# Threshold attention and a max-out FFN on one core: 29 half tiles are masked by GpSimd, and the written order is made anew

## The chip, the cores and the metric

The kernel runs on one core of one Trainium2 chip. The core has a matrix engine (TensorE, PE in the profile; its weight loads are listed apart as PEld), VectorE (DVE), ScalarE (ACT), GpSimd (POOL) and a queue engine (SyncE, SP) that here issues nearly all DMAs. All engines run their own instruction queue in order and wait for each other through semaphores. The metric is the device time of one execution in microseconds; lower is better.

## The reference, cut to what matters

```python
# q, k, v: (8, 8, 576, 64); x: 4608 tokens x 512; d_ff = 768
scores = q @ k.T / sqrt(64)                     # per batch and head, 576 x 576
thresh = max(scores, axis=-1) - tau             # tau = 0.02
scores = where(scores >= thresh, scores, -1e9)
attn   = exp(scores - max(scores)) / (sum + 1e-9)
attn_out = attn @ v
x = attn_out.transpose(0, 2, 1, 3).reshape(4608, 512)
h = max(x @ w1, x @ w2, x @ w3)
out = h @ w_out
```

Every row of a 576 x 576 score matrix keeps only the entries within tau of its maximum; the others get weight zero.

## The kernel before, in words

**Tiling.** A batch has two quads of four heads; the 16 quads run one after the other. A quad's scores are made in 9 steps of two half tiles each, so there are 288 half tiles of 128 rows x 576 columns, float32, each in one of four PSUM slots of two banks. Each half tile is a letter S in the written order. Quads' q and k are loaded (l), transposed on TensorE (T) and copied out (a on ScalarE, c on VectorE); GpSimd makes a copy of q with the partition halves exchanged (q). A finished quad gives products with v (O, copied out by w and x), and a finished batch goes through the FFN: 18 hidden pieces (six blocks of d_ff by three weights; F starts one, B is its second half) whose running maximum is made by h on ScalarE and v on VectorE, then output pieces (F, B again; copied out by u, stored by o) and the piece of the ninth rows (N, j, i). The last batch is cut in two parts (SPLIT), and its last output is copied by VectorE (f) and stored from ScalarE's queue (d).

**What happens to a half tile.** Letter m, VectorE: one pass from PSUM into a buffer z in SBUF, negated, with the row minimum nm collected, that is minus the row maximum. Then it depends on the digit of the half tile in the table MASKED:

- kind 0: s, VectorE, 128 x 1: threshold th = max - tau. e, ScalarE: Prelu(z + th) with a slope of 2^-100 for what is kept, so that kept entries are tiny and the others are large. n, ScalarE: Exp with scale -2^100, the sum collected.
- kind 1: e, ScalarE: Exp(-z + nm). k, VectorE: one pass that keeps what is at least exp(-tau) and sums it.
- kinds 2 and 3 are 0 and 1 with e reading the scores from PSUM.

When both halves of a step have their sums, r takes the reciprocals (VectorE), p normalizes each half into the bfloat16 tile P (GpSimd, one pass per half), and t transposes P through a DMA into ptq for the products.

**Buffers.** z has nine buffers of its own and, from half tile 72 on, two of eleven are taken from the two weight-staging tiles ("stage" in the profile). P has six. hm, the running maximum of the FFN, has three.

**Order.** ORDER is a text in which each letter issues one step; S, T, O, F and N carry the PSUM slot. Each engine gets its instructions in the order of this text, and `_Ordered` fixes that order. So the text decides what stands ahead of what in each queue. It is written by a planner outside the kernel, which is not shown. Nearly all instructions go through one helper, so the profile puts them on line 93; they are told apart by tile names: sc scores, z and stage the half tiles, P, ptq, tp transposes, qt, kt, qs the operands, o products, xt their copies, ph hidden pieces, hm and hT, po output pieces, ob their copies.

Of the kernel before, what the change touches and what calls it, by code (L numbers as in the profile page):

```python
# [21 lines left out]
FLAT = 2.0 ** -100  # L22

MASKED = """
220202110002002100110000100020020312000112012010100000000010100000001100
001000111010000101100000000000110001100000011110110200100000100010000000
110001101110100100010000001001100100000100101111102300000100100000001000
001000110100100001000000000100100001011110100011011100002100001000001013
"""


# [6 lines left out]
SPLIT = {7: ((0, 1), (2, 3, 4))}
# [3 lines left out]
ytS1erkpT2agmnT3pclesqS2aqetS0meqlrnspmS1eqsT2nmpS3tnrcS0zlemS2eprmS3npmtS0npsgS1sermpS2emyS3eptmT0eplmS1ayl  # L42
meS0kynS2tssT3snkynkercperlT3pmnpmntqremS0lasprgeT3pmeS2psstnplnS0mzecesqrmS3etqkeS2gpnmS1npsmtnS0prmleS3pmS
2npsmnS0yrsmetperS2epmO1eqtnkplemnzswT2teS3rplS1empnmS3tpnssrS1klepS0mapermtS2epmT1S3nmqtnkO2qemncpS3txrskT1
peS2rmeS0ptmegpamS2npS1ertsmpnlkzS2elmS3eS0mpnlO1srkepsmnO2tyeprgwnpmT1xS3cpeS0sszmF2eS1meBqkF0ngqT3shrsmBay
S2tvpnF3rpemS1BpemF0pnsvT2BnyctS1esrlsT2mphS3lezS1maF0myntpT2sS3ngrcqF1eBmpnS2svpBnrmS3peS0tmeyF2zmnF3lBsvep
S0rhkBptesF2mgeS1zvF0nsmBpteBsrgvpnF1kS3phS2semBnqmF0S3evqF2ntrmBpelS1spvBnlmS3qhF0rsmepS1tnBpsmS3ezvS2eS1rm
pF0etsyO3mnlkngpO2eswetkBxrmpT3nF2rvpaS1BnqmS0hspS3meF2prS1smntBzesmF3ezvT0tBeclT1yS2pnvS0apsmtS3eyrmlS1epS2
mepF0mnqsmnS3tkBnkeF1restpkumeS2prtBumlperkpS0ustS2umS3pesmS1eqtT0mO2nlpceqsrmO3ntywelkS0pxlS1meF3prnS2smBye
myF0thpskS1oeBpF2nlvF3nlrmBpeBkpS1hstsvS0eF3lrmpnF2mBepBsveF1nT0vBtarkS3lhqS2smleF0prF1mnBysntBveS2plvnS0pom  # L50
F3nyS1pmeBsysmF0thT2rrlpeS1clF3epsmBnqT2svBaS1evqS2nmF0pS3nmqBtnmT2pS1hrcpS3esmS0petF2melS1rmpBnF3skpetF0sve
BlBmnF2vhtF1esrBkpnS0vtT3npBmS2arvpS0ermO3eqtsmepT1swntpS0cF2epesmtnS3kT1nS0mtBessrkpameS3preS1mS0uqmuS3mpnS
1tsmS2pnoS0rempS3lempO1lnkqlemO2lnymeO0srkpetkeF3swxykxpT2BercnprtS1uyS2upmF0termqS3eBymN2lhsskpelkS0eF3ertm
S1pjBlmeS0plvF2npS1mnyF3tpmnBsopT0nvBaS1kF2ieqrssmS0hlpBmelT1qF3snrvF0epcBlepS2vBnpsmtS1nS3rmphS2mnpF1smeS0B
snmF3tevS2T0mF1atBrsekpBevS0thS2pmF3nymS1qeBrsmnpS0tvF2eplF1rmnpBskeBptF3hsvS0eBrsstpmnS1lvT2qeO0mpnlscnT3wS
1etF2srramS0lnqBmlF3eqvT1nBcpS0thF2pemS1perS3mpBnmS0ptesO1smpnkteF3yvxT0BraktyS2esS1vpeS0mpnS3meqF2mnyrmpnT0
# [12 lines left out]
ynwtprmopS0xmpS2emF3peS1mteBrsmpS0nF2pmhtS1nkBS3evF0nstmN2erkpeF1mBjpsBevS2hskF0eF3rkpteBmF1nBpveBkO2hsrvpeS
0rtwS1pnmF2npmS3eBympF1ntrvS0epBmpS2rF3svtpeS0mnpS1sBmiF2smhF0ntkBBervpS1etF3smpnF2BervpS1hsBpnmF0tevS3F1nmB  # L70
etrBkpO2vhO3nspS1xrwepS0mpF3smS2etF1snmBeBstvnS2S0veS3meF1snkeF2rmpnmpeBnkBerrptukpuO3rN1xpuO0jpuO3wptF1xpF2
hF0tvF1vF3hF0vtF1vF2hF0viF1vF2ohF0voF1vF3hF2vF1vF3hF2vO1vO0wF2xF3F1huF0vF3vF2ohF1vF3vF2hF0vF1vF3hF0vF2vF3hF1
vF2vF0hF1vF2vF0uF1ouN0ofjdi
"""


# [28 lines left out]
def kernel(  # L105
# [273 lines left out]
    def exponents(c, r):  # L379
        z = c["z", r]  # L380
        src, sign = (c[r], -1.0) if direct(c, r) else (z, 1.0)
        if masked(c["g"], c["idx"], r):
            scalar.activation(out=z, in_=src, func=AF.Exp, bias=c["nm", r], scale=-sign)
        else:
            th = c["nm", r] if direct(c, r) else c["th", r]
            scalar.activation(out=z, in_=src, func=AF.Prelu, bias=th, scale=sign, alpha=FLAT)

    def numerators(c, r):
        z, acc = c["z", r], c["sm"][:, r:r + 1]
# [89 lines left out]
    def ffn(b, part):  # L479
# [219 lines left out]
    def flow(what, fn):  # L699
        while True:  # L700
# [7 lines left out]
    line = {k: [] for k in "menkrptahvuxwcqsjf"}  # L708
# [10 lines left out]
    def issue(what, where):  # L719
# [27 lines left out]
        elif what == "m":  # L747
            c, r = line["m"].pop(0)
            maximum(c, r)
            line["e"].append((c, r))  # L750
            if not masked(c["g"], c["idx"], r) and not direct(c, r):
                line["s"].append((c, r))
        elif what == "s":
            threshold(*line["s"].pop(0))
        elif what == "e":
            c, r = line["e"].pop(0)
            exponents(c, r)
            line["k" if masked(c["g"], c["idx"], r) else "n"].append((c, r))
        elif what in "nk":
            c, r = line[what].pop(0)  # L760
            if "sm" not in c:
                c["sm"] = small.tile([128, 2], F32, name="sm")
            else:
                c["summed"] = True
# [65 lines left out]
```

## Time and profile before

| | before |
|---|---|
| time, median of 3 runs | 442.97 us (442.29 to 443.37) |
| the profiled execution: span from first to last instruction | 440.2 us |
| TensorE busy, share of the span | 418.9 us, 95% |
| VectorE | 393.9 us, 89% |
| ScalarE | 403.6 us, 92% |
| GpSimd | 317.0 us, 72% |
| mean granted TensorE clock | 0.988 |

The profile gives the execution's span; what lies around it is not in the profile, and the median of the runs is 2.77 us above the span. "Busy" is time in which an engine executes an instruction; matmuls are pipelined and their ends are modelled. A row of the stretches has an engine's busy time in that stretch and, in brackets, its instructions. A row of the waits names who waited, for whom, the total in us, how often, and the longest. A row of a group of instructions has count, busy time, mean duration in ns, and the idle time before them with what ended it. A row of the timeline has start, length, engine, line, operation, output and inputs, and the count of like instructions merged into it.

### The profile page before, as it was taken

To read this page: it belongs to the slowest core of one execution; us is meant where nothing else is said; L and a number is where in the kernel's file an instruction comes from. 1 tells how busy PE (TensorE), PEld (TensorE's weight loads), DVE (VectorE), ACT (ScalarE), POOL (GpSimd) and SP (SyncE) were. 2 spreads that over 40 slices of the span, in tenths; PEclk is the share of its full clock that TensorE was granted. 3 is DMA by queue.
4 is the path that set the end of the run, shared out by engine and by line. 5 is a ranking of instruction groups with operands and counts; after the bars stand their busy time and mean duration, and the time that the engine had idled before them with its cause. 6 is when DMAs were issued, how large, how long until landed. Compare 5 with 4: busy or idle time off the path is not lost.

```text
span 440.2 us, 14283 instructions
## 1 busy us (share of the span) xinstructions
PE 418.9 (95%) x5188; PEld 313.6 (71%) x5190; DVE 393.9 (89%) x1248; ACT 403.6 (92%) x834; POOL 317.0 (72%) x420
## 2 busy tenths in 40 slices
PE   7696789999999999999999999999999999999996
PEld 6353446787788776787678777887688777786873
DVE  4888899999999999999999999999889999998542
ACT  4999999999999999999999999999999998989521
POOL 1988999998787778867786778886585776554400
PEclk9987999999999999999999999999999999999999
DMA  6999999999999999999999999999698778583812
GB/s 190 276 239 214 270 215 260 263 252 252 220 277 224 237 165 242 291 160 232 189 242 238 202 182 273 192 199 208 135 237 153 147 109 185 102 169 72 192 50 85
DMA packets 213959, 88.50 MB, mean 201 GB/s; under 512 B 189184, under 2 KB 202240, under 8 KB 213888
## 3 DMA queue, kind: packets, MB, share of 16 engines
q1 hardware_dynamic: 213360, 86.96, 95.4%
q8 instruction: 41, 0.67, 0.6%
q10 hardware_dynamic: 528, 0.62, 0.5%
q14 instruction: 30, 0.25, 0.2%
HBM read 35.65 MB, written 9.44 MB: 102 GB/s over the span
## 4 chain that ended last, share of the span: by engine, by line
PE 78%; DVE 5%; POOL 5%; issue 4%; ACT 3%; DMA 2%; SPq 1%; DVEq 0%; POOLq 0%; ACTq 0%
PE ph L93 31%; PE sc L93 26%; PE po L93 10%; PE o L93 8%; POOL P L93 4%; PE tp L93 3%; ACT z L93 3%; DVE z L93 3%; DMA qm<-in_q_dram 2%; SPq L93 1%; DVE kt L93 1%; POOL w L93 1%; DVE stage L93 0%; DVE hm L93 0%; POOL qs L93 0%
## 5 line engine op out<-in xcount | busy, mean ns | idle before, releaser
L93 POOL TENSOR_SCALAR P<-z,rs 128x576 bf16<-128x576 f32 x250 | 202.0, 819 | 59.1 <-DVE rs L93 30.4
L93 DVE TENSOR_SCALAR_CACHE_REDUCE z<-sc 128x576 f32<-128x576 f32 x250 | 183.2, 749 | 12.2 <-PE sc L93 8.1
L93 PE MATMUL sc<-kt,qs 64*128 64x256 f32 (+2 forms) x640 | 179.8, 417 | 5.5 <-DVE z L93 3.9
L93 PE MATMUL sc<-kt,qt 64*128 64x320 f32 (+2 forms) x640 | 180.9, 429 | 3.1 <-DVE z L93 1.2
L93 PE MATMUL ph<-xt,w 64*128 64x288 bf16 (+2 forms) x2160 | 172.0, 283 | 0.2 <-DVE hm L93 0.2
L93 PEld LDWEIGHTS <-w 64*128 64x128 bf16 (+1 forms) x2160 | 128.0, 94 | 31.6 <-issue 4.0
L93 ACT ACTIVATE z<-z,th 128x576 f32<-128x576 f32 x161 | 120.5, 767 | 2.2 <-DVE th L93 1.9
L93 ACT ACTIVATE z<-z 128x576 f32<-128x576 f32 x175 | 117.6, 674 | 0.2
L93 PEld LDWEIGHTS sc<-kt,qs 64*128 64x128 f32 (+1 forms) x640 | 92.4, 179 | 22.5 <-DVE z L93 8.6
L93 PEld LDWEIGHTS sc<-kt,qt 64*128 64x128 f32 (+1 forms) x640 | 92.0, 179 | 14.7 <-DVE z L93 3.5
L93 DVE SCALAR_TENSOR_TENSOR z<-z 128x576 f32<-128x576 f32 x75 | 61.7, 827 | 1.4 <-ACT z L93 1.1
L93 POOL COPY qs<-qt 64x640 f32<-64x640 f32 (+3 forms) x66 | 45.9, 695 | 19.5 <-ACT qt L93 16.1
L93 ACT ACTIVATE z<-z,nm 128x576 f32<-128x576 f32 x72 | 53.9, 767 | 0.0
L93 PE MATMUL po<-wo,hT 64*128 64x512 bf16 (+3 forms) x454 | 53.3, 354 | 0.3
L93 DVE TENSOR_TENSOR hm<-ph,hm 128x576 bf16<-128x576 f32 (+2 forms) x54 | 37.0, 685 | 9.8 <-PE ph L93 9.6
L93 ACT ACTIVATE hm<-ph 128x576 bf16<-128x576 f32 (+2 forms) x54 | 31.9, 590 | 14.3 <-PE ph L93 13.8
L93 PEld LDWEIGHTS <-hT 64*128 64x128 bf16 (+2 forms) x456 | 28.4, 95 | 18.5 <-issue 2.6
L93 DVE TENSOR_TENSOR hT<-ph,hm 128x576 bf16<-128x576 f32 (+2 forms) x54 | 36.9, 683 | 2.8 <-PE ph L93 1.0
L93 PE MATMUL o<-ptq,vb 128*64 128x512 bf16 (+2 forms) x544 | 38.7, 282 | 0.2 <-DVE z L93 0.2
L93 POOL TENSOR_SCALAR P<-stage,rs 128x576 bf16<-128x576 f32 x38 | 29.5, 783 | 11.7 <-DVE rs L93 8.4
L93 ACT ACTIVATION_READ_ACCUMULATOR z<-z 128x1 f32 x175 | 33.6, 192 | 0.0
L93 PEld LDWEIGHTS <-vb 128*64 128x64 bf16 x544 | 22.4, 111 | 14.0 <-issue 5.6
(44 smaller groups left out, 412.2 us busy)
## 6 DMA issues: line engine op xcount, KB each, us to landing
vm<-in_v_dram SPq DMA_DIRECT2D x32, 256.0 KB, 4.6
qm<-in_q_dram SPq DMA_DIRECT2D x15, 512.0 KB, 4.7
km<-in_k_dram SPq DMA_DIRECT2D x15, 512.0 KB, 5.4
out_dram<-ob SPq DMA_DIRECT2D x14, 512.0 KB, 4.5
stage<-in_moe_w_dram SPq DMA_DIRECT2D x9, 512.0 KB, 5.6
ptq<-P SPq DMA_TRANSPOSE x144, 4.5
vr<-in_v_dram SPq DMA_DIRECT2D x16, 128.0 KB, 3.8
stage<-in_moe_w_out_dram SPq DMA_DIRECT2D x3, 512.0 KB, 5.5
```

The lines of the kernel that those rows point to most:

```text
L93: ins = fn(*a, **kw)
```

## The change

29 half tiles get a new kind, 4. For it m and s are as for kind 0. Then GpSimd makes two passes: b computes (z + th) * 2^100 and writes it as 8-bit integers to the upper byte of each element of a bfloat16 tile "far" whose lower bytes are zero, so that an element is either a very large number or minus zero; C adds far to z. G, ScalarE, is then a single Exp(-z + nm) with the sum collected. There is one far tile. The table MASKED and the whole text ORDER are new; they were made by the planner with instruction fetches taken into account and with larger random late landings of DMAs. hm has two buffers instead of three. The first half tile of kind 4 is number 82 of 288.

| kind | before | after |
|---|---|---|
| 0 | 187 | 173 |
| 1 | 84 | 69 |
| 2 | 14 | 13 |
| 3 | 3 | 4 |
| 4 | 0 | 29 |

```diff
 MASKED = """
-220202110002002100110000100020020312000112012010100000000010100000001100
...
+221202110000002100110001300030022312000012012010010001000000110100001001
+100001101040100000110440000000000140000400101011001140000001001004000004
...
 PBUFS = 6
+FARS = 1
+FAR = 2.0 ** 100
...
 ORDER = """
-lllllllllT0laqqlcT1aS2lcqqgmS0S3lemS1lmnT2lmeS3lsaS0mnqlqemT3lyerclcapsnS1lS2eqmlS3qemznmS2perS1mnpsmnpT3ske
...
-vF2vF0hF1vF2vF0uF1ouN0ofjdi
+llllllllllT0lacT3qqlaS0lqqcmgS1S3lemS2lmnS0lmelS3elmT1lacqeslmS1qS0ngkyT2lermlacqS1emqnpmS2epS0rsmnS1ptmS2np
...
+1uF3hoF2vF1vF0hF2vF3vF1hF0vF2vF3hF0vF1vF2hF3vF1vF2hF3vF0vF3uoN0uoF1jifd
...
+    def on_pool(c, r):
+        return by_mask[2 * number[c["g"], c["idx"]] + r] == "4"
...
     def exponents(c, r):
...
+        if on_pool(c, r):
+            scalar.activation(out=z, in_=z, func=AF.Exp, bias=c["nm", r], scale=-1.0, accum_out=summed(c)[:, r:r + 1])
+            return
...
+    far = [one.tile([128, S], BF16, name=f"far{x}") for x in range(FARS)]
+    for t in far:
+        vector.memset(t, 0.0)
+    fars = iter(range(1 << 20))
+
+    def marked(c, r):
+        c["far", r] = t = far[next(fars) % FARS]
+        pool.tensor_scalar(out=t.bitcast(mybir.dt.int8).rearrange("p (n x) -> p n x", x=2)[:, :, 1],
+                           in0=c["z", r], scalar1=c["th", r], scalar2=FAR, op0=OP.add, op1=OP.mult)
+
+    def moved(c, r):
+        pool.tensor_tensor(out=c["z", r], in0=c["z", r], in1=c["far", r], op=OP.add)
...
-                    st["hm", f] = hp_.tile([128, nr, n], BF16, name="hm", bufs=3)
+                    st["hm", f] = hp_.tile([128, nr, n], BF16, name="hm", bufs=2)
...
         elif what == "m":
             c, r = line["m"].pop(0)
             maximum(c, r)
-            line["e"].append((c, r))
+            if not on_pool(c, r):
+                line["e"].append((c, r))
...
         elif what == "s":
-            threshold(*line["s"].pop(0))
+            c, r = line["s"].pop(0)
+            threshold(c, r)
+            if on_pool(c, r):
+                line["b"].append((c, r))
+        elif what == "G":
+            exponents(*line["G"].pop(0))
+        elif what == "b":
+            c, r = line["b"].pop(0)
+            marked(c, r)
+            line["C"].append((c, r))
+        elif what == "C":
+            c, r = line["C"].pop(0)
+            moved(c, r)
+            line["G"].append((c, r))
```

The place where the sum tile is made moves into a helper, `summed`, that G uses too.

More of the change, by code (lines that the diff above doesn't have):

```diff
@@ L24 @@
 MASKED = """
-220202110002002100110000100020020312000112012010100000000010100000001100
-001000111010000101100000000000110001100000011110110200100000100010000000
-110001101110100100010000001001100100000100101111102300000100100000001000
-001000110100100001000000000100100001011110100011011100002100001000001013
+221202110000002100110001300030022312000012012010010001000000110100001001
+100001101040100000110440000000000140000400101011001140000001001004000004
+010014001010100100100140000400140040000000101101411014000001400000041400
+200040010001100400400040000001400000101111401100011004000400140041224131
 """
@@ L36 @@
 PBUFS = 6
[L38 removed]
+FARS = 1
+FAR = 2.0 ** 100
+SPLIT = {7: ((0, 1), (2, 3, 4),)}
 ORDER = """
[L41 to L44 removed]
@@ new lines @@
+ngsnlrmptamS3eqT2kS1npS0ssnrrmptemS3pempemlqeslcS3nptT1meS0zS2rnktT3passrmnS1pmeptkeS2qnmlpesrS1cgnpS0smteqm
+epkeymnS2trS3eprmeS1pmnT0ptkS2eymnpmeT1znsrS3cS2pgasmS1tnpS0meqO3ssrtempnkpT1S2nwarrmpetS1mpeS3mpetT2scS1nzm
+S2epmnO0erkpnS1mtezrsxklpeS0mlnS3plsmeS1lpS2remlpO0nslmylnpmO3tewqerkS2pxS1smeF3qnBkpF0ntrssmBhpS2revqF1eF3m
+ytBeS0pnvBgnpmS1tS2nprmT0epslmF1hpgBkaF3teqssvBesrS1vpnS2mpnT0F3meyS1qtsceS2ynrsS0mpnBmpF1hmtzBersS2veptS3mn
+zS1mnT0F2lpmeBgrasF3sktpeF1vBepklBhS2qgeT0vF3lyermF1eBcpBnkpS0hsS2rnmS1zemS0pgnsmO2tqemnyrspF0veBszwteS1vS3e
@@ new lines @@
+pT2mnS0lpmS1agrkF3npS2meBqmeO0zrnssmekpS1gxF2tsvnS0pmeF3ymBpteBrkqhT1F0nscS2ptervS1peBmT3zntmS2avzS1nmT3elS0
+pmS2tpsrF1smepmetqS0sekS2pntsBmebmetS0rscpF2umuplnkS1CleBslmnlrkpeS0lS1utmpO3usGrsmpnO0sqwnprlkeS3lpS1xmtS2e
+pF0rmnS3ymBeS1myepF2tsshmF3ybnBrkS0nCtvBeF1smepT2BvaptF0khS2pnS3srlmF1eplBmGbF2lsrvnBlpBservtCT3hS0ceS1tmpnF
+2qsT0meBpS3savS1GpmS0lnpF2mlF3eqsrlsS1rmepBtnsmF0pBnvqtBhsrS1pevF2pnS3mBqtnmS0yeF1rsmoS3eyBvtpnF0mphT2Bnscpt
+S3evF1bS2esrmCF0emBnF3spvBnspktBhS1pevF2S0etrmpT3GBmpS1arssvptnO0mpnesbT3twS2ncCF1oemlS3rnsplS2emlByqmlnpGT0
@@ new lines @@
+sS2qaS3emS0urrmpO2ukesmS1ytxS3emT2yS0nlympO1elcpelsmO3pelwtqesrkS0qxS2etmF1pnkpnS0mS3nrmpT2eBsmatbkeS0CS2urr
+smN3epmupnstkS0epF1mS2jlpBsnslmF0qhlkS3eylBsmeF2lvF1GtypBrnrS3yvetpBmS2phS0rsnmpT3F1ecpF2ntsBmpeS3vqS0ntsmpB
+emS1eF3tvS0esmBnF2meS1rkhpBmnF0T3pnvBS1tarsssprvF2eF3pmelBbkoS0hS1tpsrmeBCF2nsmF0evBpnS1vqtBGmT3qF2hrsS1cple
+BslpmnS3pntsO0vnprmepF2orswT3blBaS0tCvnS3meF1pS2meBpnstmF0qT3hsBcGpS2vS1etO3rempnmqS0kxyS1nmF2eT3ssBmpaS0rye
+tsrvyS3pnmS1qlS2emF0plembtnmT1BpscelCkeiS3uF1kpulnmS0lqGBtmsrrrspS3kuS2epmO0upmtespS1ewS2pnmT3pO0aktersmpnS3
@@ new lines @@
+S1tsqxrmS2eyS0monF3mplF1emByetBpsskhF2peS0voBelrmF3pnlS1vptnBsmbS0hF2kCeS3mnBrsS1semtyqF0nmpF3evBpeF1vBtnkBh
+rS2ssGpvS3npmF0eS1rtrmpF2nsmBpeBrspstvS3hS1bemF2peT0mBpetcF3nT1CvBalS0svnS2pmF1nqtF3mGbBskBhCS2evS0T1nmqS3ls
+mO2elsrsGlrcpO0nmpesrptrwS1xbS3emT0F2CnsmS1aBspmeF3vT0pGtBsecpS2S1hrptmF0npF3smeBptnT2vBpaS1rvynS0tsmeS3yS2m
+qnF1meyplsermlqS0nT3lS2pmnlBqcetmpeS0rpkuS2lupO3lsmnlpmeO0lqwetsrknbS3S1xkS2epmF0epmteS3CmBsrkepF1mtuS2pusrB
+pmtS3hbS0emT1opF2maS3onkqBtGF1ssskN0CemevqnBrrS3sjpvF2GikpF0nS1mBeptmBhpsS3rrevS1pteS2mpS0nmytF3nsmF1npsBmeB
@@ new lines @@
+pvT2eF0btssrchS3pnBmS1pevF2yeT3CsmBnlS0vtaS1emqT2F3nclqF0snlkByBlhmS2erF3sspmeS1pBveF2btGvF0CBnmS3hrrrS1spnm
+BGF2pvT3ptBsmaF0pervS3bS1tskeBCmO2hmepS0GwpF3nrmS1ptnBssmpF0evS2ptnS1rspmeBS3mpetS2snsmbO1nrspveS3mptxS0myeS
+1F2esmyCnmS0nrsBpemqtnsT0puS1cuS3yGmpoO0elrmpnlO2wpetkqnS3sT0eF1ymlarrsxkqS3nT2BmeqlcelpS0srlupF2ntmS3puBsbm
+eS0S1hCmF3oeF2sstmnpBeBpvS1npF0vGS3bmBnkCF2htF1srsrmT0BpatBveqS0eS3vpS2nmptF1GmT0pBnssrmqF3thBscbeT2F1vpaF0e
+rspS3nBCtmBevS3hqS2rnsmpF0emF3pGBssptS2evS1qnmBpnS0mF2tevS1rBmpS3hmS0pnsF2srmtpnF1mByepS3rssveS0ytbmeBO2nvpe
@@ new lines @@
+kCF1nwT3nBrcpS2hmF3ptGT1mpBarssS2sptveT0pF1meT3qcBtaS2eqvT0S3nmqS1emqF2nsrcpnS3mpS0erkS1pteBmepmnF3tmuskebS1
+sekS0CuBrrmeompnS2S1upmS0upmeO2osGkekS3yteO1mxsrrysmepO0weptkS3yxS2pemF1ptnS0mF3pnkBetS2srrmhpBnmF1pF0evptBn
+sskBpS3ekN2hbtrmprsF3evpS0jBCtnmF1nF2svpBiGBpervO3pthS0wnpS2mtS1mF3S0srsmebF2mBnCBssveS0F1pGvS3eprmF2nBptmBh
+psS3nvF0bteS1rmpF2sBmpeBCstvS3nF1hmS0eBsmbGO2knO3CxS0rrweS2vpGF3mpF1meBptkBepF0hrvF2nptBnBpvS3trS1vpS0mpF2sm
+tbS3meCF1emkGBrkpBupuoN2utuO0eO1jkoO3xirwF2pxF1hpF0vF3tvF1hF2vF0vF1hF3vF2vF1hF3vF0vF1hF2vF3vF0hF1vO2vO0wF2xF
@@ L386, in exponents, with summed @@
             scalar.activation(out=z, in_=src, func=AF.Prelu, bias=th, scale=sign, alpha=FLAT)
+    far = [one.tile([128, S], BF16, name=f"far{x}") for x in range(FARS)]
[8 more added lines that the diff above has]
+        pool.tensor_tensor(out=c["z", r], in0=c["z", r], in1=c["far", r], op=OP.add)
+    def summed(c):
+        if "sm" in c:
+            c["summed"] = True
+        else:
+            c["sm"] = small.tile([128, 2], F32, name="sm")
+        return c["sm"]
     def numerators(c, r):
-        z, acc = c["z", r], c["sm"][:, r:r + 1]
+        z, acc = c["z", r], summed(c)[:, r:r + 1]
         if masked(c["g"], c["idx"], r):
@@ L707 @@
                 O=products(), F=pieces(), N=iter(lambda: ninths.pop(0), None))
-    line = {k: [] for k in "menkrptahvuxwcqsjf"}
+    line = {k: [] for k in "menkrptahvuxwcqsjfbCG"}
     casts = iter([w[1] for w in wl])
@@ L760, in issue @@
             c, r = line[what].pop(0)
[L761 to L764, printed above, removed]
             numerators(c, r)
```

29 lines of the change are left out of this document (1 added, 28 removed).

## The prediction

> **What bounds the kernel now.** I read the page's busy shares first, then five stretches of the span, then the waits of TensorE in the first stretch and behind it, and last single instructions for their true spacing.
>
> ```profile
> span 440.2 us, 14283 instructions
> ...
> PE 418.9 (95%) x5188; PEld 313.6 (71%) x5190; DVE 393.9 (89%) x1248; ACT 403.6 (92%) x834; POOL 317.0 (72%) x420
> ```
>
> ```profile
> core 0: us, PE busy (x) PEld busy (x) DVE busy (x) ACT busy (x) POOL busy (x), PEclk, DMA share, GB/s
> 0.00:8.00 8.00, 6.07 (x66) 5.36 (x68) 2.08 (x9) 2.38 (x4) 1.73 (x8) 1.00 0.57 148
> 8.00:71.00 63.00, 48.61 (x438) 28.29 (x436) 55.55 (x187) 61.70 (x132) 55.99 (x73) 0.92 1.14 245
> 71.00:96.00 25.00, 24.43 (x336) 19.51 (x333) 23.77 (x79) 24.67 (x53) 23.12 (x32) 1.00 1.19 258
> 96.00:402.00 306.00, 305.60 (x4024) 236.48 (x4023) 293.82 (x932) 298.71 (x611) 229.80 (x301) 1.00 1.00 202
> 402.00:440.00 38.00, 34.16 (x337) 23.93 (x336) 18.66 (x45) 16.12 (x37) 6.30 (x8) 1.00 0.36 97
> ```
>
> The cuts are at the first FFN matmul and near the start of the last scores:
>
> ```profile
> 71.32 0.65 PE L93 MATMUL ph<-xt,w 64*128 64x288 bf16 x8
> ```
>
> Two regimes show. Up to 71 us there is no FFN to fill TensorE: it is busy 48.61 of 63 us, while ScalarE is busy 61.70 of 63. There ScalarE sets the pace and TensorE waits for banks to be emptied. From 71 us on TensorE is busy without a hole (305.60 of 306), and ScalarE (298.71) and VectorE (293.82) run just behind it. GpSimd has 306 - 229.80 = 76.2 us free there. The waits tell the same:
>
> ```profile
> PE sc L93 <- DVE z L93: 5.1, 9, 1.2
> PEld sc L93 <- DVE z L93: 10.4, 14, 1.4
> ```
>
> These are of the first 71 us; TensorE's own and its weight loads' from 72 us to the end are
>
> ```profile
> PE tp L93 <- DMA qm<-in_q_dram: 0.4, 1, 0.4
> PE ph L93 <- DVE hm L93: 0.2, 1, 0.2
> ...
> PEld L93 <- issue: 10.7, 35, 0.4
> ...
> PEld sc L93 <- DVE z L93: 1.7, 6, 0.3
> PEld sc L93 <- ACT z L93: 1.1, 3, 0.4
> ...
> PEld sc L93 <- ACT qt L93: 1.0, 3, 0.5
> PEld sc L93 <- DVE hm L93: 0.9, 4, 0.3
> ```
>
> So behind 72 us the matmuls wait 0.6 us in all, and these weight-load waits on VectorE and ScalarE add to 4.7 us, partly beside running matmuls. That is about all that relief of VectorE and ScalarE can buy there.
>
> **The change, part by part.** Counting marks: unmasked halves of kind 0 go from 187 to 173, kind 1 (VectorE masks) from 84 to 69, kind 2 from 14 to 13, kind 3 from 3 to 4, and 29 are of the new kind 4. No kind 4 stands among the first 82 half tiles, so the new passes do not touch the first regime. Rows that price a half tile:
>
> ```profile
> 255.87 0.76 ACT L93 ACTIVATE z<-z,th 128x576 f32<-128x576 f32 x1
> 256.53 0.67 ACT L93 ACTIVATE z<-z 128x576 f32<-128x576 f32 x1
> 257.11 0.19 ACT L93 ACTIVATION_READ_ACCUMULATOR z<-z 128x1 f32 x1
> 257.20 0.67 ACT L93 ACTIVATE stage<-stage 128x576 f32<-128x576 f32 x1
> ...
> 301.56 0.74 DVE L93 SCALAR_TENSOR_TENSOR z<-z 128x576 f32<-128x576 f32 x1
> 302.22 0.08 DVE L93 DVE_READ_ACCUMULATOR z<-z 128x1 f32 x1
> ```
>
> Instructions overlap, so I price by distance from start to start. Prelu takes 256.53 - 255.87 = 0.66 us, an Exp with its accumulator read 257.20 - 256.53 = 0.67, of which the read is 0.09. The masking pass of VectorE takes 302.22 - 301.56 = 0.66. An Exp with a bias and no accumulation I take as the Prelu with a bias, 0.66.
>
> - ScalarE: 15 fewer Prelu+Exp pairs (kinds 0 and 2: 201 to 186), -15 x 1.33 = -20.0; 14 fewer lone Exp (kinds 1 and 3: 87 to 73), -14 x 0.66 = -9.2; 29 new Exp with bias and read (letter G), 29 x 0.75 = +21.8. Sum -7.4 us.
> - VectorE: -14 x 0.66 = -9.2; 15 more thresholds (187 to 202) at most 0.14 each by the row below, +2.1. Sum -7.1 us.
> - GpSimd: 29 times two passes over 576 elements. The trace has one-input passes only:
>
> ```profile
> L93 DVE TENSOR_SCALAR th<-nm 128x1 f32<-128x1 f32 x187 | 25.4, 144 | 0.2
> L93 POOL TENSOR_SCALAR P<-z,rs 128x576 bf16<-128x576 f32 x250 | 202.0, 819 | 59.1 <-DVE rs L93 30.4 <-issue 5.6 <-DVE th L93 4.9
> ```
>
> Its shortest, median and longest are in a view of that tile:
>
> ```profile
> L93 POOL TENSOR_SCALAR P<-z,rs x250: 734/744/1891, 13.0 to 411.6; 128x576 bf16<-128x576 f32 x125
> ```
>
> The first pass (float to every second byte) is a tensor-by-scalar pass with two operations like P: 0.744. The second reads two tensors. Lower bound of the pair: 2 x 0.744 = 1.49; upper: 0.819, P's mean by the page, plus P's longest, 1.891, so 2.71. I take 0.744 + 2 x 0.744 = 2.23, because a second input is at worst a second reading, and P is the nearest row. 29 x 2.23 = 64.7 us, and 229.8 + 64.7 = 294.5 of 306: 96% full, hidden, but barely. Cover ends at 76.2 / 29 = 2.63 us per pair.
>
> The Trainium skill, page "GPSIMD Engine Reference", section 3.1, gives 2.6 cycles per element for a two-input pass, 4497 ns for 2048 elements. By that the second pass is an estimated 1.27 us, the pair 2.01, the sum 58.3 and GpSimd 94% full; its section 4.1 speaks against doing such work there at all. No row of this trace has a two-input pass on GpSimd.
>
> - New waits: ScalarE's G waits for the second GpSimd pass; behind G stand the Prelus and Exps of other half tiles, and behind those VectorE's reciprocals and TensorE's banks. Counted over the written order, each TensorE piece at its usual length in the trace, G stands on average 3.1 us of TensorE work behind its second pass, in the tightest cases 1.1 to 1.6. Some ten of 29 may wait a few tenths of a microsecond, 3 us of ScalarE, inside the 7.4 it is given back. P passes behind the new ones start later; by the same count there are 11.1 us of TensorE work between maximum and P instead of 11.7, so the buffers of z, 9 and two, do not get short by plan. Free POOL time is the cover; without it see the second rival.
> - Far tile: one memset of 128x576 bf16 on VectorE ahead of those that the warm-up waits for. TensorE's transposes start 0.25 us after the warm-up ends:
>
> ```profile
> 0.83 0.83 DVE L93 MEMSET vr<- 128x128 uint32 x5 [0.83 <-PEq L811]
> 1.05 3.58 PE L93 MATMUL warm<-vr 128*128 128x128 bf16 x36 [1.05 <-DVE vr L93]
> 4.88 0.24 PE L93 MATMUL tp<-identf,qm 64*128 64x64 f32 x1 [0.25 <-DMA qm<-in_q_dram]
> ```
>
>   The five memsets take 0.83 us together, so one more is about 0.2 to 0.35: at most +0.1. Taken as 0.
> - hm with two buffers instead of three: each new hm waits for the last maximum of the one two before, which in the order is always issued earlier; 0, and if VectorE were late by a piece, 0.5 us once.
> - The order. I compared both texts up to the first F. Both have the same TensorE pieces before it: 54 S, 16 T, 4 O; so the same matmuls follow it. But 33 second Exps (n) stand before it instead of 36, with 50 e's in both; k, VectorE's, is 14 instead of 12. ScalarE is the bound there (61.70 of 63), so the first F comes 3 x 0.67 = 2.0 us earlier, at 69.3. Bounds: 0, if TensorE or GpSimd (55.99 of 63) take over; 4.0, the six fewer ScalarE passes (27 n's against 31, 39 e's against 41) ahead of the 36th P, which ends batch 0. VectorE gets +2 k = 1.3 us on 55.55 of 63: hidden.
> - DMAs: the same 104 loads, 144 transposes and stores, moved by a few places on SP's queue. Instruction fetches: the 10.7 us of weight loads that wait for "issue" are the only trace of them that I can name; TensorE's instructions are the same in number, so 0.
> - The end: the last output piece now follows the ninth-row piece. Before, ScalarE's queue issued the last two stores at 436.36 and 0.65 later; after, the last one can go when VectorE's copy (0.69) behind the last matmul is done, at about 437.0 too: 0.
>
> ```profile
> 435.52 0.69 DVE L93 COPY ob<-po 128x512 f32<-128x512 f32 x1 [3.27 <-PE po L93]
> 436.30 0.38 ACT L93 ACTIVATE ob<-po 128x256 f32<-128x256 f32 x1 [1.43 <-PE po L93]
> 436.36 1.29 ACTq L93 DMA_DIRECT2D out_dram<-ob  x2
> ```
>
> Behind the first F, relief of ScalarE and VectorE by 7 us each removes some of the 4.7 us of waits; I take -0.6. Sum: 440.2 - 2.0 - 0.6 = 437.6 us of span. The profiled span of 440.2 lies 2.77 under the median of 442.97, and I add that: 440.4.
>
> **The rivals.**
> Same time, 442.9. TensorE behind 71 us is full, so the relief of ScalarE and VectorE is worth nothing; and the 2.0 us at the front are lost to another wait there, GpSimd's most likely. For it: 305.60 of 306, and GpSimd at 55.99 of 63 early. Against it: fewer n's before the first F are a plain count.
>
> Slower, 446.9: GpSimd becomes the bound from half tile 82 on. It decides from 2.63 us per pair. At 2.85 the passes cost 82.7, GpSimd needs 312.5 of 306, and 6.5 us are added to 440.4. For it: beside VectorE's two-input masking pass a P takes far longer than 0.744:
>
> ```profile
> 301.74 1.17 POOL L93 TENSOR_SCALAR P<-z,rs 128x576 bf16<-128x576 f32 x1 [0.75 <-DVE rs L93]
> ```
>
> It ran while the pass of 301.56 did. Also, GpSimd's free time is mostly waiting for sums, which a full queue cannot simply use. Against it: 14 of those masking passes go away, and early on GpSimd ran 89% full (55.99 of 63) with ScalarE still at 98%. On the same page, sections 1 and 8, the Trainium skill says that GpSimd's SBUF interfaces are shared with VectorE's two-input instructions; the row of 301.74 agrees.
>
> Faster by more, 437.0: of the 4.7 us of weight-load waits and their like 4.0 go, not 0.6. For it: ScalarE falls from 298.71 to about 291 of 306. Against it: those waits run beside matmuls.
>
> **How the numbers follow.** Forecast 440.4 (own range 438.5 to 441.6): 0.42. Faster by more: 0.10. Same: 0.22. Slower: 0.26. A difference under 0.3%, 1.3 us, cannot be told from none here. So faster 0.52, same 0.22, slower 0.26. The range goes from the deep case to a little beyond the slow one, 436.8 to 447.5.
>
> **What would show it.** First FFN matmul at 69 to 70 us; TensorE busy over 99% from there on; ScalarE's busy time down by about 7 us, VectorE's by 7 to 10; GpSimd at 380 us in all and over 90% between 96 and 402; the two-input pass at 1.2 to 1.5 us. The prediction is wrong if the first F is not earlier, if waits of ScalarE for GpSimd's z add up to more than 5 us, or if VectorE's waits for P behind 72 us grow by several times from
>
> ```profile
> DVE z L93 <- POOL P L93: 0.7, 3, 0.3
> ```

## The result and the profile after

The changed kernel is slower: 455.72 us median of four runs (452.81 to 458.77) against 443.17 beside it (442.29 to 444.62). The ratio over all runs is 1.030, 95% interval 1.024 to 1.035; it is not the quotient of the two medians, which is 1.028. The forecast was 440.4 with a range to 447.5. The profiled execution took 452.81 at a span of 450.9, so 1.9 us lie around the span. The page after, first lines:

```profile
span 450.9 us, 14304 instructions
...
PE 428.4 (95%) x5190; PEld 313.3 (69%) x5190; DVE 400.9 (89%) x1236; ACT 399.4 (89%) x833; POOL 377.6 (84%) x478
```

Four of the five stretches shown of before:

```profile
8.00:71.00 63.00, 49.28 (x434) 30.37 (x430) 58.53 (x189) 59.72 (x124) 55.17 (x72) 0.86 1.07 233
71.00:96.00 25.00, 24.41 (x320) 17.52 (x320) 23.31 (x72) 23.68 (x49) 22.73 (x29) 1.00 1.09 224
96.00:402.00 306.00, 303.84 (x3904) 227.24 (x3902) 289.48 (x899) 291.20 (x609) 282.20 (x354) 1.00 1.02 204
402.00:450.00 48.00, 44.53 (x484) 32.70 (x478) 27.22 (x70) 22.45 (x49) 15.65 (x18) 0.99 0.40 98
```

The first FFN matmul in its timeline:

```profile
72.01 2.60 PE L95 MATMUL ph<-xt,w 64*128 64x288 bf16 x32
```

GpSimd's total is as forecast (377.6 against 380) and so is its share of the long stretch (282.20 of 306, 92%, where over 90% was forecast). TensorE too is over 99% busy there (303.84 of 306), as forecast. Two things are not. The first F is at 72.01, not at 69 to 70. And VectorE, which has 14 masking passes fewer, is busy 400.9 us and was busy 393.9. Of the 10.7 us added to the span, 9.5 are in TensorE's *busy* time (428.4 against 418.9) with the same number of matmuls but for two: it is still "full", and slower, at a granted clock of 1.00 from 71 to 402 us as before. The groups of instructions on the page of before, and then of after, show where it stands, in the score matmuls:

```profile
L93 PE MATMUL sc<-kt,qs 64*128 64x256 f32 (+2 forms) x640 | 179.8, 417 | 5.5 <-DVE z L93 3.9
L93 PE MATMUL sc<-kt,qt 64*128 64x320 f32 (+2 forms) x640 | 180.9, 429 | 3.1 <-DVE z L93 1.2
```

```profile
L95 PE MATMUL sc<-kt,qt 64*128 64x320 f32 (+2 forms) x640 | 186.0, 438 | 7.3 <-DVE z L95 3.9
L95 PE MATMUL sc<-kt,qs 64*128 64x256 f32 (+2 forms) x640 | 185.7, 426 | 3.8 <-DVE z L95 2.6
```

The two groups are busy 371.7 us instead of 360.7, 11.0 more for the same 1280 matmuls; the idle time before them goes from 8.6 to 11.1, most of it behind VectorE. Now the two engines that share the masking. Groups of before, then of after (busy, mean ns, idle time before):

```profile
L93 DVE SCALAR_TENSOR_TENSOR z<-z 128x576 f32<-128x576 f32 x75 | 61.7, 827 | 1.4 <-ACT z L93 1.1
...
L93 POOL TENSOR_SCALAR P<-stage,rs 128x576 bf16<-128x576 f32 x38 | 29.5, 783 | 11.7 <-DVE rs L93 8.4 <-ACT z L93 0.8 <-POOL vr L93 0.7
...
L93 DVE SCALAR_TENSOR_TENSOR stage<-stage 128x576 f32<-128x576 f32 x12 | 9.6, 804 | 0.0
```

```profile
L95 POOL TENSOR_SCALAR P<-z,rs 128x576 bf16<-128x576 f32 x250 | 196.7, 798 | 17.7 <-DVE rs L95 7.5 <-ACT z L95 2.0 <-DVE th L95 1.5
...
L95 DVE SCALAR_TENSOR_TENSOR z<-z 128x576 f32<-128x576 f32 x67 | 64.0, 957 | 2.8 <-ACT z L95 2.8
...
L95 POOL TENSOR_SCALAR P<-stage,rs 128x576 bf16<-128x576 f32 x38 | 30.4, 807 | 3.9 <-ACT z L95 1.5 <-POOL qs L95 1.0 <-POOL vr L95 0.8
...
L95 POOL TENSOR_TENSOR z<-z,far 128x576 f32<-128x576 f32 x20 | 28.0, 1400 | 1.1
...
L95 POOL TENSOR_SCALAR far<-z,th 128x576 int8<-128x576 f32 x20 | 14.9, 748 | 3.3 <-DVE th L95 1.6
...
L95 POOL TENSOR_TENSOR stage<-stage,far 128x576 f32<-128x576 f32 x9 | 13.2, 1465 | 0.3
...
L95 DVE SCALAR_TENSOR_TENSOR stage<-stage 128x576 f32<-128x576 f32 x6 | 8.7, 1442 | 0.0
L95 POOL TENSOR_SCALAR far<-stage,th 128x576 int8<-128x576 f32 x9 | 8.6, 953 | 2.7 <-DVE th L95 1.8 <-DVE rs L95 0.3
```

The GpSimd pair costs (28.0 + 14.9 + 13.2 + 8.6) / 29 = 2.23 us. That is the forecast to the hundredth, but by luck, as the run with one-input masking will show. What did not follow the forecast is VectorE's side: its masking passes, 87 before for 71.3 us, are now 73 for 72.7 us: the relief has gone into longer passes. By the timelines, before, 9 of 87 took over 1.0 us, the longest 1.43; after, 27 of 73, up to 2.30. Two places of the timeline of after show how:

```profile
277.79 1.28 POOL L95 TENSOR_TENSOR stage<-stage,far 128x576 f32<-128x576 f32 x1
277.84 1.84 DVE L95 SCALAR_TENSOR_TENSOR stage<-stage 128x576 f32<-128x576 f32 x1
279.04 1.25 POOL L95 TENSOR_SCALAR P<-z,rs 128x576 bf16<-128x576 f32 x1
```

```profile
231.70 0.28 POOL L95 CAST vr<-vr 64x128 bf16<-64x128 f32 x1
231.73 2.30 DVE L95 SCALAR_TENSOR_TENSOR stage<-stage 128x576 f32<-128x576 f32 x1
...
231.96 1.46 POOL L95 TENSOR_SCALAR P<-z,rs 128x576 bf16<-128x576 f32 x2
...
233.96 0.75 DVE L95 TENSOR_TENSOR hm<-ph,hm 128x576 bf16<-128x576 f32 x1
...
234.76 0.53 PE L95 MATMUL sc<-kt,qt 64*128 64x320 f32 x1 [0.63 <-DVE hm L95]
```

In the first, VectorE starts 0.05 us after GpSimd's add and ends 0.61 us after the add does: it did its work behind it. The next P, begun in that time, takes 1.25 us instead of 0.74. They take turns. In the second, VectorE comes 0.03 us behind a cast of GpSimd's, stands through the rest of it (0.25 us) and through both P's, and ends 0.61 us after the last of them. The running maximum hm behind it is late, and TensorE idles 0.63 us for hm. The Trainium skill, page "SBUF — State Buffer", section "SBUF: two separate sides", says that VectorE's instructions with two SBUF inputs and GpSimd's that read SBUF take the shared port pair exclusively for a whole instruction while the other blocks. Both places agree with it, and at 231.73 the wait lasts over three GpSimd instructions, two of which began after VectorE's.

GpSimd's results are not late, as the waits from 72 us on say:

```profile
POOL far L95 <- DVE th L95: 3.4, 4, 1.4
PEld L95 <- PE ph L95: 3.0, 8, 0.4
...
DVE z L95 <- POOL P L95: 1.1, 2, 0.6
...
ACT stage L95 <- POOL stage L95: 0.8, 2, 0.6
```

### The profile page after: what moved, and what is told of

It is laid out like the page before. It is cut to its first block, busy times and chain, and to the rows that moved or that the text cites. A ratio compares the mean times of both kernels' runs of the same rounds, so it can differ in the third digit from the quotient of the medians.

```text
span 450.9 us, 14304 instructions
## 1 busy us (share of the span) xinstructions
PE 428.4 (95%) x5190; PEld 313.3 (69%) x5190; DVE 400.9 (89%) x1236; ACT 399.4 (89%) x833; POOL 377.6 (84%) x478
## 4 chain that ended last, share of the span: by engine, by line
PE 74%; DVE 13%; issue 4%; POOL 4%; ACT 4%; DVEq 0%; POOLq 0%; ACTq 0%
PE sc L95 27%; PE ph L95 25%; PE po L95 10%; DVE z L95 9%; PE o L95 8%; PE tp L95 3%; POOL P L95 3%; ACT z L95 3%; DVE stage L95 1%; PE warm L95 1%; DVE hm L95 1%; DVE hT L95 1%; DVE kt L95 1%; DVE rs L95 0%; DVE th L95 0%
## 5 line engine op out<-in xcount | busy, mean ns | idle before, releaser
L95 POOL TENSOR_SCALAR P<-z,rs 128x576 bf16<-128x576 f32 x250 | 196.7, 798 | 17.7 <-DVE rs L95 7.5
L95 PE MATMUL sc<-kt,qt 64*128 64x320 f32 (+2 forms) x640 | 186.0, 438 | 7.3 <-DVE z L95 3.9
L95 PE MATMUL sc<-kt,qs 64*128 64x256 f32 (+2 forms) x640 | 185.7, 426 | 3.8 <-DVE z L95 2.6
L95 PEld LDWEIGHTS <-w 64*128 64x128 bf16 (+1 forms) x2160 | 123.6, 94 | 34.2 <-issue 4.6
L95 ACT ACTIVATE z<-z,th 128x576 f32<-128x576 f32 x150 | 112.4, 767 | 8.2 <-DVE th L95 5.7
L95 PEld LDWEIGHTS sc<-kt,qt 64*128 64x128 f32 (+1 forms) x640 | 93.7, 181 | 24.8 <-DVE z L95 10.1
L95 ACT ACTIVATE z<-z 128x576 f32<-128x576 f32 x163 | 109.5, 673 | 0.4
L95 DVE SCALAR_TENSOR_TENSOR z<-z 128x576 f32<-128x576 f32 x67 | 64.0, 957 | 2.8 <-ACT z L95 2.8
L95 ACT ACTIVATE z<-z,nm 128x576 f32<-128x576 f32 x83 | 63.0, 766 | 3.0 <-DVE z L95 2.8
L95 DVE TENSOR_TENSOR hm<-ph,hm 128x576 bf16<-128x576 f32 (+2 forms) x54 | 37.1, 686 | 11.1 <-PE ph L95 9.9
L95 PE MATMUL o<-ptq,vb 128*64 128x64 bf16 (+2 forms) x544 | 38.5, 282 | 0.3 <-DVE z L95 0.3
L95 ACT ACTIVATION_READ_ACCUMULATOR z<-z 128x1 f32 x163 | 31.2, 191 | 0.0
```

Source lines behind the costliest of these rows:

```text
L95: ins = fn(*a, **kw)
```

## The experiments

Theory: two costs add up, GpSimd's passes colliding with VectorE's two-input masking passes, and the new written order by itself. Rival: GpSimd is the bound, by the number and length of its passes. Ratios are to the kernel before, measured beside each run, and are over all fast runs; times are medians. The two can differ by up to 0.4%, so differences of a few us between runs of different sets are good to 1 or 2 us.

**No passes.** The calls `marked(c, r)` and `moved(c, r)` are taken out of after; the 29 half tiles of kind 4 stay unmasked.

> The changed kernel without the two GpSimd passes: the 29 half tiles of kind 4 go unmasked, all else and the whole order stay. Theories: (A) a fuller GpSimd holds up VectorE's two-input masking passes, and through them banks and hm; (B) GpSimd's queue is simply too full, so P and G come late; (C) the new order itself is worse, whatever GpSimd does. A and B expect 441 to 445 us, VectorE's masking passes back at a mean of 0.80 to 0.85 us from 0.96; C expects 452 to 457.

Measured: 451.59 us, ratio 1.022 (1.019 to 1.025). Without a single new pass, most of the loss is there: the passes cost about 4 us. The time lies 0.4 us below the range named for the new order as the cause, and far above that of the other two theories. VectorE's 73 masking passes took 66.4 us, 6.3 less than in after.

**One input.** Another second pass, so that only its two-tensor form goes; kind 4 stays unmasked.

```diff
-        pool.tensor_tensor(out=c["z", r], in0=c["z", r], in1=c["far", r], op=OP.add)
+        for n in (S, 384):
+            pool.tensor_scalar(out=c["z", r][:, 0:n], in0=c["z", r][:, 0:n], scalar1=1.0, scalar2=1.0, op0=OP.mult, op1=OP.mult)
```

> The changed kernel with the second GpSimd pass (two tensors in, 1.28 us) replaced by two passes with one tensor in, 576 and 384 elements, about 1.25 us together; the 29 half tiles go unmasked. Same load of GpSimd, no second input. If it is the two-input pass on GpSimd that collides with VectorE's masking passes: 444 to 448 us. If any GpSimd pass collides with them (A), or the full queue is what counts (B), or the order (C): 452 to 457, the masking passes still at 0.9 us or more.

Measured: 453.72, ratio 1.027 (1.023 to 1.030); the masking passes 71.7 us. So it is not the two-tensor form on GpSimd: its passes with one tensor input collide too, as P does.

**Mask1 after.** VectorE's masking pass of kinds 1 and 3 becomes a pass with one tensor input (73 half tiles unmasked); GpSimd's passes stay.

```diff
-            vector.scalar_tensor_tensor(out=z, in0=z, scalar=thr, in1=z,
-                                        op0=OP.is_ge, op1=OP.mult, accum_out=acc)
+            vector.tensor_scalar(out=z, in0=z, scalar1=1.0, scalar2=None,
+                                 op0=OP.mult, op1=OP.add, accum_out=acc)
```

> The changed kernel with VectorE's masking pass (kinds 1 and 3) replaced by a pass with one tensor in and the sum collected; those 73 half tiles go unmasked. GpSimd's passes, its load and the order stay. A expects the 73 passes at 0.75 us or less and 442 to 447 us; B and C expect 451 to 457, with only a little less VectorE time.

Measured: 448.81, ratio 1.015 (1.010 to 1.021), 6.9 us less than after. Its groups:

```profile
L95 POOL TENSOR_SCALAR P<-z,rs 128x576 bf16<-128x576 f32 x250 | 183.3, 745 | 32.6 <-DVE rs L95 12.9 <-DMA ptq<-P 5.4 <-DVE th L95 4.2
...
L95 DVE TENSOR_SCALAR_CACHE_REDUCE z<-z 128x576 f32<-128x576 f32 x67 | 49.6, 743 | 3.6 <-ACT z L95 3.6
...
L95 POOL TENSOR_SCALAR P<-stage,rs 128x576 bf16<-128x576 f32 x38 | 28.0, 746 | 5.0 <-issue 2.5 <-DMA ptq<-P 1.0 <-POOL qs L95 0.5
...
L95 POOL TENSOR_TENSOR z<-z,far 128x576 f32<-128x576 f32 x20 | 25.6, 1280 | 1.1
...
L95 DVE TENSOR_SCALAR_CACHE_REDUCE stage<-stage 128x576 f32<-128x576 f32 x6 | 4.5, 744 | 0.3 <-ACT stage L95 0.3
```

All lengthening is gone, on both engines: P's mean is 745 ns, the add's 1280. The score matmuls are back at 182.1 + 181.5 = 363.6 us from 371.7. So these rows are the prices without collisions; VectorE's is that of another instruction, but the shortest masking passes of after took 0.73 us as well. Against them, collisions took 72.7 - 54.1 = 18.6 us of VectorE in after, 227.1 - 211.3 = 15.8 in P and 64.7 - 58.8 = 5.9 in the new pairs (the add over stage and both far passes took 11.5, 15.0 and 6.7 here). In before they were already there, 71.3 - 87 x 0.741 = 6.8 on VectorE and 231.5 - 211.3 = 20.2 in P: in the old order it was mostly GpSimd that waited.

**Pairs in before.** Before with 29 pairs of dummy GpSimd passes, one behind every seventh P from the 82nd on, and two hm buffers.

> The kernel before with 29 pairs of GpSimd passes like the new ones, on tiles that nobody waits for, one behind every seventh P from the 82nd on; masks, order and all else stay, but hm has two buffers. A: the 87 masking passes of VectorE go from 0.82 to 0.95 us or more, 448 to 455 us. B: P is later, no slower masking passes, 444 to 448. C: 442 to 444.

Measured: 467.53, ratio 1.058 (1.055 to 1.061). Its long stretch, and then two of its waits from 72 us on:

```profile
96.00:402.00 306.00, 291.11 (x3681) 218.90 (x3679) 282.48 (x861) 279.29 (x567) 270.99 (x334) 0.99 0.90 191
```

```profile
DVE z L93 <- POOL P L93: 11.4, 14, 1.9
...
PEld sc L93 <- DVE z L93: 6.5, 15, 2.0
```

GpSimd is at 270.99 of 306, less than in after, and yet VectorE waits 11.4 us for P. The masking passes took 81.9 us instead of 71.3. The time lies above the ranges of all three theories (448 to 455 at most). An order in which no room was left for the pairs pays far more than the new one: GpSimd's free time was not free where they fell. The two hm buffers are a second difference; in this trace ScalarE's copies into hm wait for TensorE only, so no wait for a buffer shows, but how much of the 25 us is whose was not followed.

**Order alone, and mask1 before.** The new order without the GpSimd passes and with one-input masking, and the old order with one-input masking: the two edits above together, and the second in before. Nothing collides in either.

> The changed kernel without the two GpSimd passes and with VectorE's masking pass replaced by a pass with one tensor in: GpSimd light, nothing to collide with, all masked half tiles of kinds 1, 3 and 4 go unmasked. What is left over 442 us is the written order alone. The run without the passes gave 451.6, the run with one-input masking 448.8. If both costs add (order plus collisions): 445 to 447 us. If the collisions are only a small part and the order is nearly all (C): 448 to 451. If collisions are all that the order adds (A): 440 to 443.

> The kernel before with VectorE's masking pass replaced by a pass with one tensor in; its 87 half tiles of kinds 1 and 3 go unmasked. Its masking passes average 0.82 us against 0.75 at best, 6 us in all, mostly on no path. If the collisions cost time in the old order too (A, in both): 437 to 440 us. If they cost only where GpSimd is full or the order lets them meet: 441 to 443.

Measured: order alone 447.05 (11 runs), ratio 1.010 (1.007 to 1.013); mask1 before 440.69, ratio 0.998 (0.994 to 1.001). Without collisions the new text is 6.4 us slower than the old one. That is the text together with what came with it: the new table of kinds, two hm buffers and the far tile. By the medians collisions cost the old order 1.5 us, which cannot be told from none, as the interval includes 1; in the new one the two-input passes alone cost 451.59 - 447.05 = 4.5, and some 5 by the ratios.

**B apart, and order b apart.** In eight places of the new text a B follows its own F at once, which the old text nowhere has; each shows a weight load waiting some 0.4 us (the 3.0 us, 8 times, quoted above). The eight B's are moved behind the next TensorE piece, in after and in order alone.

```diff
-S2epmnO0erkpnS1mtezrsxklpeS0mlnS3plsmeS1lpS2remlpO0nslmylnpmO3tewqerkS2pxS1smeF3qnBkpF0ntrssmBhpS2revqF1eF3m
+S2epmnO0erkpnS1mtezrsxklpeS0mlnS3plsmeS1lpS2remlpO0nslmylnpmO3tewqerkS2pxS1smeF3qnkpF0BntrssmhpS2BrevqF1eF3m
...
```

> The changed kernel with one edit in the text: at the 8 places where the second half of an FFN piece (B) stands directly behind its own first half (F), B moves behind the next TensorE piece; the text before had no such place. In the trace each of the 8 costs 0.22 us more than other first halves, while the weight load waits for the first half's matmuls. If these waits are on the path: 1.8 us less than the changed kernel, 453 to 454.5 against about 455. If TensorE makes it up elsewhere: no change.

> The run of the order alone (no GpSimd passes, one-input masking), with the 8 B's moved behind the next TensorE piece. If the 8 waits are part of what the order costs: 1.5 to 2 us below the order alone. If they are not: the same time.

Measured: 454.36, ratio 1.025 (1.019 to 1.030), and 448.35, ratio 1.010 (1.006 to 1.015). No gain that can be told from none: order alone has 1.010 with and without the edit. In after, the intervals leave room for the 1.8 us that was expected if the waits are on the path.

**Mask1 front, mask1 back.** One-input masking in after only for the 25 half tiles ahead of number 82 (`if 2 * number[...] + r < 82`), or only for the 48 from there on; those stay unmasked.

> The changed kernel with one-input masking on VectorE for the 25 half tiles of kinds 1 and 3 ahead of number 82, where no GpSimd pass of the new kind stands; they go unmasked. With one-input masking everywhere the first FFN piece came at 68.6 to 69.7 us instead of 72.0, and the whole was 6.9 us shorter. If the early collisions alone cost the front: first FFN piece at about 69, and 452 to 453.5 us if ScalarE-bound work up to the next products takes part of it back, 449 to 450 if the collisions there are all of the 6.9.

> The same for the 48 half tiles of kinds 1 and 3 from number 82 on, which share their time with the new GpSimd passes; they go unmasked. First FFN piece still at 72. If the collisions behind half tile 82 cost most of the 6.9 us: 449 to 451 us. If those in front do: 453 to 455.

**After again** is the changed kernel once more, beside these two.

> The changed kernel as it is, on the same chip as the runs beside it, and a second profile of it. All theories: 453 to 457 us, first FFN piece at 71 to 73 us, VectorE's 73 masking passes at a mean of 0.95 to 1.0 us.

Measured: front 452.45, ratio 1.023 (1.019 to 1.028); back 450.2, ratio 1.018 (1.013 to 1.023); after again 455.47, ratio 1.030 (1.026 to 1.035). Taking the collisions out ahead of number 82 is worth 3.0 us (the intervals still overlap), behind it 5.3, both 6.7: the parts don't quite add. When pieces start, by the timelines' matmuls in the order of the text (us; the piece is named by its letter and count):

| | first F | F 21 | F 40 | S 264 | end of span |
|---|---|---|---|---|---|
| before | 71.32 | 123.18 | 167.44 | 364.66 | 440.23 |
| order alone | 68.64 | 124.31 | 169.01 | 367.67 | 444.32 |
| mask1 after | 69.66 | 125.50 | 173.60 | 371.63 | 448.56 |
| mask1 front | 69.65 | 126.36 | 171.28 | 371.76 | 449.75 |
| mask1 back | 74.33 | 130.25 | 174.95 | 372.70 | 449.64 |
| after | 72.01 | 127.39 | 172.62 | 372.87 | 450.88 |

Mask1 front has the first F 2.4 us earlier than after, and ends 1.1 earlier. Mask1 back has it 2.3 us later, and ends 1.2 earlier. So a shift at the first F does not carry to the end. Nor is it all due to the edit: up to the first F mask1 back is the same program as after, and two traces of after have it at 72.01, so executions differ by over 2 us there. Over all traces the picture holds. With the old text ahead of the first F it lies at 71.1 to 71.5, whether masking has two inputs (two traces) or one (three, mask1 before at 71.50). With the new text and two-input masking it lies at 72.0 to 74.3 (seven traces), and with one-input masking at 68.6 to 69.7 in six of eight. The other two are to 180 new at 72.24, where TensorE waits 3.33 us for a load on the way (see below), and order km early at 71.42, for which no reason was found. Nor is it TensorE's granted clock: up to 71 us it is 0.86 in after and 0.92 in before, but 0.86 in mask1 front too, which has the first F at 69.65.

Order alone shows where the lead goes: 2.7 us ahead of before at the first F, 1.1 behind at F 21. The stretches up to the first F and from there to F 21, of before and of order alone:

```profile
8.00:71.30 63.30, 48.91 (x440) 28.48 (x438) 55.85 (x190) 62.00 (x132) 56.29 (x74) 0.92 1.14 245
71.30:123.20 51.90, 51.33 (x660) 40.89 (x658) 49.14 (x160) 51.35 (x107) 46.48 (x61) 1.00 1.19 244
```

```profile
8.00:68.60 60.60, 46.89 (x442) 29.26 (x440) 55.85 (x192) 59.79 (x126) 51.06 (x74) 0.94 1.05 241
68.60:124.30 55.70, 54.03 (x662) 37.58 (x660) 51.22 (x166) 53.23 (x111) 44.62 (x62) 1.00 1.11 238
```

ScalarE works 62.00 + 51.35 = 113.4 us up to F 21 in the one and 59.79 + 53.23 = 113.0 in the other: the work taken out ahead of the first F comes behind it, and in before ScalarE is busy 51.35 of 51.90 there. By these shares the part in which ScalarE sets the pace ends near 123 us, not at 71, and that is where the lead is lost. This reading rests on busy shares, and TensorE's is as high there (51.33). It does not explain the 1.1 us that order alone loses beyond its lead: there ScalarE has 2.5 us free.

**Order alone hm3.** Order alone with three hm buffers and no far tile.

> The order alone (no GpSimd passes, one-input masking) with three buffers of hm as before, without the far tile. If two buffers of hm are part of what the order costs: 1 us or more below the 447.05 of the order alone. If not: the same within 1 us.

Measured: 445.8, ratio 1.008 (1.005 to 1.012). The intervals overlap: that hm has a part in it can neither be shown nor excluded.

**Hybrids of the two texts.** With one-input masking and without the passes, cut where both texts have issued the same TensorE pieces: at half tile 90 (some 121 us) or 180 (some 250 us).

> The text and table of after up to half tile 90 and FFN piece 20 (about 121 us), those of before from there on; one half tile of kind 4 is left. As in order alone no GpSimd passes for kind 4 (its half tile stays unmasked) and a one-input pass in place of VectorE's masking pass (its half tiles stay unmasked), two hm buffers. The old order in this form took 440.7, the new one 447.0. If the order's cost is made in the first 121 us (ScalarE-bound start, three fewer n's before the first F but no gain by FFN piece 21): 446 to 447. If it is made behind: 441, or 440 if the earlier first F at 68.6 to 69.6 is kept. If it is spread evenly: 442.5.

> The reverse: before's text and table up to half tile 90 and FFN piece 20, after's behind it, 28 of kind 4; otherwise as order alone. If the cost is made in the first 121 us: 441. If behind: 446 to 447. If spread evenly over the span: 445.

> After's text and table up to half tile 180 and FFN piece 74 (about 250 us), before's behind it, 13 of kind 4; otherwise as order alone. Cost in the first 121 us or in 121 to 250: 446 to 447. Cost behind 250: 441. Spread evenly: 444.

> The reverse: before's text and table up to half tile 180, after's behind, 16 of kind 4; otherwise as order alone. Cost in the first 250 us: 441. Cost behind 250: 446 to 447. Spread evenly: 443.5.

Measured: front new 445.44, ratio 1.006 (1.003 to 1.010); rest new 448.03, 1.013 (1.010 to 1.016); to 180 new 448.93, 1.014 (1.011 to 1.018); from 180 new 448.67, 1.013 (1.009 to 1.016). Every mixture is slower than the pure old text (0.998), and three of four are no faster than the pure new one (1.010). If the stretches simply added, front and rest would come to 1.2% together over the old text; they come to (1.006 - 0.998) + (1.013 - 0.998) = 2.3%, which would put each seam at about half a per cent. The pair cut at 180 comes to (1.014 - 0.998) + (1.013 - 0.998) = 3.1%, nearly 1% for each seam, so even that is no constant. The experiment can't place the order's cost; no stretch of the new text pays when put into the old one.

**Km early, and order km early.** The trace of to 180 new has the longest wait of TensorE for a load in any of these traces, in its timeline:

```profile
53.06 0.46 PE L94 MATMUL tp<-identf,km 64*128 64x64 f32 x8 [3.33 <-DMA km<-in_k_dram]
```

The new text issues this load of k 5.0 to 7.1 us ahead of its use, the old one 9.3 to 10.2. Its letter is moved up, in after and in order alone:

```diff
-pempemlqeslcS3nptT1meS0zS2rnktT3passrmnS1pmeptkeS2qnmlpesrS1cgnpS
+pempemlqesllcS3nptT1meS0zS2rnktT3passrmnS1pmeptkeS2qnmpesrS1cgnpS
```

> After, whole, with one load moved: the fragment of k for the sixth half quad is issued directly behind the load of q ahead of it, and not behind three transposes of P more. In the traces of the new text it is issued 5.0 to 7.1 us before TensorE's transposes need it, in those of the old text 9.3 to 10.2; one run of the new text (to 180 new) waited 3.33 us for it at 53.06. If such late landings are what makes most executions of after longer than the profiled one (452.8 against a median of 455.5) and part of what the order costs: median 452.5 to 453.5, a spread under 3 us instead of 6. If not: 455 to 456 with the spread of before.

> Order alone (no GpSimd passes for kind 4, one-input pass in place of VectorE's masking pass, all those half tiles unmasked) with the same load moved. Order alone took 447.05 with runs from 445.2 to 450.2. If the late load is part of the order's cost: 445 to 445.7 and no run over 448. If not: 446.5 to 447.5 with the same spread.

Measured: 454.28, ratio 1.028 (1.025 to 1.031), runs from 452.4 to 456.8; and 451.15, ratio 1.018 (1.014 to 1.022), which is slower than order alone; why was not followed. The load is now issued at 41.50, and its use comes no earlier, but waits for something else, in the timeline of km early:

```profile
53.97 0.47 PE L95 MATMUL tp<-identf,km 64*128 64x64 f32 x8 [2.47 <-DVE z L95]
```

So nothing shows the late load to be the order's cost. The profiled execution of km early was a long one (span 454.2). Against after it is 1.2 us later at the first F, 1.9 at F 21, 3.1 at F 40 (175.68), and then no more than 3.3 to the end. That is one trace of how a long execution comes about: in small steps in the first 170 us. Why, it does not show.

## Why the prediction was wrong

- **The first F, 2.0 us earlier and carried to the end: failed twice.** The count of Exps fits where nothing collides: six of eight traces have the first F at 68.6 to 69.7, 1.8 to 2.9 us ahead of mask1 before. With collisions it is at 72.01. Two k's more were priced at 1.3 us of VectorE and called hidden; by the timelines the 14 masking passes ahead of the first F took 14.2 us and the 12 of before 10.1, so 4.1 more. And the gain would not have lasted: the prediction ended the ScalarE-bound part at the first F because TensorE is "305.60 of 306" behind it. TensorE's busy time rose by 9.5 us with the same matmuls, so being full was no proof that it set the pace. The step should have counted ScalarE's work up to 123 us, where it comes out even.
- **VectorE -7.1 us: failed.** It became +7.0. Not all of that is work: VectorE's groups add up to 472.2 us before and 472.7 after, and the rest of the 7.0 is neighbours that overlap less in the profile. But no relief is left. Masking passes were priced at 0.66 from one row and GpSimd's new time was priced only on GpSimd. The second rival quoted the row that shows the collision (a P of 1.17 us beside a masking pass) and the rule behind it, but used it for GpSimd's length alone. Its other side, VectorE standing still while GpSimd runs, is what acted: 18.6 us of VectorE time against 6.8 before. In time, taking those collisions out is worth 455.47 - 448.81 = 6.7 us.
- **The order, priced at 0: failed.** It costs 4.8 us against before, and 6.4 with the same masking. By its trace against that of before, which has two-input masking: -2.7 up to the first F, +3.8 to F 21, +0.4 to F 40, +1.4 to S 264, +1.1 behind. "The same TensorE pieces before the first F" was true and said little. Neither the eight B's nor the load of k could be shown to have a part in it, and hm's buffers are undecided. Which steps of the text cost it stays open.
- **The GpSimd pair, 2.23 us: right as a price, by luck, and wrong in its parts.** Without collisions it is 0.748 + 1.28 = 2.03 us, and 5.9 / 29 = 0.20 is collision. The second pass takes 1.28, within the 1.2 to 1.5 named, and not the 1.49 of the sum. The Trainium skill's page "GPSIMD Engine Reference", section 3.1, had given an estimated 1.27, and the trace agrees.
- **G's waits, at most 3 us: right.** 0.8 us on stage is the largest row of them. VectorE's waits for P went from 0.7 to 1.1 us only, so of the three signs of being wrong it was the first F that came.
- **ScalarE -7.4: -4.2** (403.6 to 399.4). Its groups add up to 473.8 us before and 467.6 after, so 6.2 less; of the 3.2 us between forecast and total, 2.0 are again neighbours that overlap less.
- **The rivals.** Slower had the right sign and the wrong mechanism: it decided from 2.63 us per pair, and the pair took 2.23. "Same" rested on a full TensorE too.
- **2.77 us around the span: 1.9** in this execution, and 1.7 to 2.0 in every run whose span is on record: the 2.77 set the median of the runs against the span of a shorter execution. The other three runs of after were 2 to 6 us longer than the profiled one, a spread that order alone has as well (445.2 to 450.2).

In sum, by medians of different sets: before 442.2, order alone +4.8, two-input masking passes beside P in that order +4.5, GpSimd's new passes +3.9, of which 448.81 - 447.05 = 1.8 is left when VectorE's passes have one input: 455.5.

## What to carry to other kernels

When work moves from one engine to another, price it on every engine that it can hold up, not only on the one that does it: look in the trace for rows of either engine that are longer than their own shortest while the other runs. A share of 99% busy doesn't name the pace-setter when the same instructions can be busy longer; count the work of the engine just behind it up to several later points, and see whether a gain is still there. A written order is a cost of its own: compare old and new order with the suspected operations taken out of both before crediting or blaming those operations.

## What the runs showed of the hardware

- VectorE's pass with two SBUF tensors and GpSimd's passes over 128x576 exclude each other, whichever comes second: 0.73 us became up to 2.30 on VectorE, and at 279.04 P's 0.74 became 1.25. With one tensor input on VectorE all 288 P's took 0.74 to 0.76 us.
- GpSimd's passes with one tensor input collide as those with two do: VectorE's masking passes take 71.7 us in all beside the one, 72.7 beside the other, 66.4 without the added passes.
- VectorE can stay blocked over several GpSimd instructions: the 2.30 us at 231.73 are 0.25 of a cast, two whole P's of 1.46 together, and 0.61 of its own.
- An 8-bit output to every second byte costs GpSimd nothing beside a bfloat16 one: 0.747 us against P's 0.744.
